# Loading a branch's register earlier, and idle matmuls in the first batch: attention and MLP on one core

## Chip, cores, metric

One core of one Trainium2 chip. The metric is the device time of one execution in microseconds (us), as the median of several; 32 of the 33 executions of the kernel before that ran beside the experiments lie within 0.3% of their median (313.96 us), and that spread is larger than most effects below, so the traces carry much of the argument. Engine names: PE is the matmul engine (PEld its weight loads), DVE VectorE, ACT ScalarE, POOL GpSimd, SP SyncE; a q behind the name is the engine's sequencer.

## The reference

```python
# q, k, v: (8, 8, 576, 64), s: (8, 8, 576); w_in: (512, 2048), w_out: (2048, 512)
scores = q @ k^T / sqrt(64)
cum    = cumsum(max(s, 0))
scores = where(causal, -1e9, scores + min(-(cum_i - cum_j), 0))
x      = (softmax(scores) @ v) as (4608, 512)
out    = gelu(x @ w_in) @ w_out            # exact gelu, float32
```

## The kernel before

The kernel computes attention in a factored form that is only right when certain bounds hold on the data. It tests them on the chip and writes the verdict, 0 or 1, to the one-element tile `bad`. At the end all engines load `bad` into a register and branch: where it is 0, as for this data, a long general version of the whole computation is skipped. The last sub-block of the output is evacuated and stored only behind the branch.

The MLP is done in nine chunks of 512 tokens, each with a layer 1 and four sub-blocks of layer 2. The end of the kernel before:

```python
        else:                                   # chunks 7 and 8
            for sub in range(4):
                l2_item(c, (sub,), store=(c, sub) < LAST)     # 16 matmuls of 512 columns each
                if c == B - 1:                                # chunk 7: writes `bad`
                    (cert_1, cert_2, cert_3, cert_4)[sub]()
    fast.close()

    rv = nc.values_load(bad[0:1, 0:1], min_val=0, max_val=1)  # register load on every engine
    with tc.If(rv > 0):
        ...                                                   # the general version, cut here
    with tc.manual_schedule():
        for sub in range(LAST[1], 4):                         # only sub-block 3 of chunk 8
            ...
            for i in range(2):
                cols = slice(i * 256, i * 256 + 256)
                nc.vector.tensor_copy(o_sb[:, cols], y[:, cols])
                nc.sync.dma_start(out=out[r0 : r0 + 128, cols], in_=o_sb[:, cols])
```

At the start PE would often be idle (in the run without the idle matmuls behind the weights it is busy for 2.54 us of the 5 from 5 to 10 us). `filler(n)` issues n matmuls of a zero tile (512 columns) into a PSUM buffer nobody reads:

```python
    filler(17)
    cum_sum(); masks(); weights()              # weights: PE transposes the cumulative sums
    ...
    filler(3)
    filler(3, raws[0, "qk"][:, 1, 0, :128])    # waits for the first key tile
    ...                                        # scores of batch 0 (sc_first: one filler behind each half)
    av_item(0, 1, 0)                           # value matmuls
    av_item(0, 1, 1)
    sc_first(1, 1, (1,), 0)
    to_xT(0, 0, True)                          # PE transposes of x; DVE copies them to xT
    to_xT(0, 1, True)
    mk_item(0, 0, 1)
    ...                                        # then layer 1 of chunk 0, which reads xT
```

## Time and profile before

| | before |
|---|---|
| median of the first 3 executions | 314.47 us (313.52 to 315.29) |
| span of the profiled execution | 313.1 us |
| PE busy | 303.3 us (97%) |
| last matmul ends / last copy starts | 307.6 / 308.20 us |

The lines are shown inside the prediction below. How to read them: a timeline line has the start in us, the length in us, the engine, the source line, the operation, what is written and read, how many instructions were merged, and in brackets how long the engine had been idle and what released it. A line of the waits has the waiter, the releaser, the total in us, the number of times and the longest. The span runs from the first to the last instruction; the time of an execution is 1.7 to 1.9 us longer than its span.

### The profile page before, as it was taken

Reading aid. Unit: us, or ns where it says so; the run is one execution under the profiler, and the core shown is the slowest. Engines: PE = TensorE matmul, PEld = TensorE weight load, DVE = VectorE, ACT = ScalarE, POOL = GpSimd, SP = SyncE. Lnnn points to the kernel's source line nnn. Section 1 sums busy time; section 2 is a strip of 40 time slices with the busy share of each in tenths; the row PEclk is TensorE's granted clock in tenths of the full one; section 3 lists DMA queues with packets and bytes.
Section 4 is the critical chain, followed back from the end, with each engine's and each line's share of the span. In section 5 each row is a group of like instructions: output and inputs, shape, how many; then the busy total and the mean of one; then the engine's idle time right before and its main releaser. Section 6 shows DMA issues by size and latency. Waiting matters only on the chain. (4 is left out here: it accounts for less than half of the span.)

```text
span 313.1 us, 6092 instructions
## 1 busy us (share of the span) xinstructions
PE 303.3 (97%) x2506; PEld 154.7 (49%) x2506; DVE 195.9 (63%) x397; ACT 193.3 (62%) x262; POOL 53.6 (17%) x72
## 2 busy tenths in 40 slices
PE   7999989999999999999999999999999999999992
PEld 2479655444554455445454445444544454444441
DVE  7876667697769785965597649954995532250010
ACT  2687868878848772965587458764876567006300
POOL 7383350142002400160006000500000000000000
PEclk9999999999999999999999999999999999999999
DMA  7999999769631973098218940634110311020012
GB/s 137 218 230 209 226 222 287 144 140 201 168 92 23 213 172 110 8 189 198 86 31 173 208 104 19 161 84 70 50 27 36 101 52 25 33 92 12 0 72 72
DMA packets 33028, 36.73 MB, mean 117 GB/s; under 512 B 17761, under 2 KB 22113, under 8 KB 32993
## 3 DMA queue, kind: packets, MB, share of 16 engines
q0 software_dynamic: 11472, 22.81, 37.3%
q1 hardware_dynamic: 20336, 12.93, 14.9%
q10 hardware_dynamic: 1184, 0.52, 0.6%
q8 instruction: 21, 0.34, 0.5%
q14 instruction: 15, 0.11, 0.1%
HBM read 36.85 MB, written 9.44 MB: 148 GB/s over the span
## 5 line engine op out<-in xcount | busy, mean ns | idle before, releaser
L488 PE MATMUL o_ps<-w_out_r,gT 128*128 128x512 bf16 x576 | 135.6, 379 | 0.8 <-DMA w_out_r<-in_moe_w_out_dram 0.8
L472 PE MATMUL h_ps<-xT,w_in_r 128*128 128x512 bf16 (+1 forms) x640 | 131.6, 358 | 0.6 <-DVE xT L418 0.6
L477 ACT ACTIVATE gT<-h_ps 128x1024 bf16<-128x1024 f32 (+1 forms) x80 | 75.1, 938 | 65.5 <-PE h_ps L472 64.4
L472 PEld LDWEIGHTS <-w_in_r 128*128 128x128 bf16 x640 | 60.0, 98 | 54.7 <-issue 0.7
L488 PEld LDWEIGHTS <-gT 128*128 128x128 bf16 x576 | 52.0, 98 | 57.7 <-issue 3.6
L364 ACT ACTIVATE P<-sc_ps 128x1024 bf16<-128x1024 f32 x56 | 54.3, 1021 | 26.1 <-PE sc_ps L349 26.1
L500 DVE COPY o_sb<-o_ps 128x512 f32<-128x512 f32 x30 | 20.7, 691 | 55.7 <-PE o_ps L488 55.7
L122 POOL DMA_DIRECT2D raw_v<-in_v_dram x39 | 33.1, 860 | 125.7 <-ACT sq L216 115.3
L188 DVE STREAM_TRANSPOSE qkT<-raw_qk 128x576 f32<-128x576 f32 x32 | 37.3, 1238 | 0.4 <-DMA raw_qk<-in_q_dram 0.3
L449 DVE RECIPROCAL rc<-av 128x4 f32<-128x4 f32 (+1 forms) x80 | 14.0, 175 | 35.1 <-PE av L440 35.0
L450 DVE TENSOR_TENSOR x<-av,rc 128x256 bf16<-128x256 f32 (+1 forms) x80 | 33.8, 423 | 3.0
L440 PEld LDWEIGHTS <-P 128*128 128x128 bf16 x576 | 26.5, 98 | 15.8 <-DVE P L372 1.4
L208 DVE TENSOR_REDUCE amx<-raw_qk 128x2 f32<-128x2304 bf16 x13 | 32.6, 2534 | 0.0
L440 PE MATMUL av<-vv,P 128*128 128x65 bf16 x576 | 30.2, 193 | 0.2 <-DVE x L450 0.2
L224 DVE TENSOR_TENSOR vv<-raw_v,wb 128x512 bf16<-128x512 f32 (+1 forms) x39 | 25.3, 691 | 4.0 <-DMA raw_v<-in_v_dram 4.0
L216 ACT ACTIVATE sq<-raw_v 128x512 bf16<-128x512 f32 (+1 forms) x40 | 24.8, 621 | 0.0
L372 DVE TENSOR_TENSOR P<-P,tri_bf 128x1024 bf16<-128x1024 bf16 (+1 forms) x33 | 22.0, 669 | 3.3 <-ACT P L364 3.2
L349 PE MATMUL sc_ps<-qkT 32*128 32x256 bf16 (+2 forms) x560 | 18.0, 250 | 0.0
L349 PEld LDWEIGHTS <-qkT 32*128 32x128 bf16 x560 | 11.7, 92 | 12.2 <-issue 8.9
L505 ACT ACT_TABLE_LOAD x8 | 10.3, 1283 | 1.3 <-PEq L823 1.2
L508 ACT ACT_TABLE_LOAD x8 | 10.3, 1283 | 0.1
L498 ACT ACTIVATE o_sb<-o_ps 128x512 f32<-128x512 f32 x5 | 2.9, 592 | 11.1 <-SPq L672 9.3
(80 smaller groups left out, 97.8 us busy)
## 6 DMA issues: line engine op xcount, KB each, us to landing
out_dram<-o_sb SPq DMA_DIRECT2D x34, 256.0 KB, 2.3
raw_v<-in_v_dram POOLq DMA_DIRECT2D x31, 256.0 KB, 5.6
raw_qk<-in_q_dram POOLq DMA_DIRECT2D x7, 576.0 KB, 7.8
raw_qk<-in_k_dram POOLq DMA_DIRECT2D x7, 576.0 KB, 11.1
w_in_r<-in_moe_w_in_dram POOLq DMA_DIRECT2D x4, 512.0 KB, 10.9
w_out_r<-in_moe_w_out_dram POOLq DMA_DIRECT2D x4, 512.0 KB, 15.9
raw_v<-in_v_dram POOLq DMA_DIRECT2D x8, 128.0 KB, 6.2
raw_qk<-in_q_dram POOLq DMA_DIRECT2D x2, 288.0 KB, 7.1
```

The source lines that it names most:

```text
L122: eng.dma_start(out=t[:n_st, st, :, :], in_=bass.AP(tensor=v.tensor, offset=v.offset + b * H * S * D + st * 128 * D, ap=[[D, n_st], [S * D ...
L188: nc.vector.transpose(qkT[b % 2][:, i, g, :S, :].rearrange("p s e -> p (s e)").bitcast(fp32) .rearrange("p (l j) -> p j l", j=LT), raws[b, ...
L208: nc.vector.tensor_reduce(amx[:, b * HG + g], raws[b, "qk"][:, :, g, :], axis=AX, op=ALU.max, apply_absolute_value=True,)
L216: nc.scalar.activation(sq[:n_st], raws[b, "v"][:n_st, st].rearrange("p h d -> p (h d)"), func=AF.Square, accum_out=sumv[:n_st, b, st : st ...
L224: eng.tensor_tensor(vv[b % 2][:n_st, st, :, 0:D], raws[b, "v"][:n_st, st, :, :], w.unsqueeze(2).to_broadcast([n_st, H, D]), op=MULT,)
L349: nc.tensor.matmul(s_ps[h // 2][:, h % 2, off : off + n], lhsT=qk[r, 1, g, jt * 128 : jt * 128 + 128, e], rhs=qk[r, 0, g, i0 : i0 + n, e], ...
L364: nc.scalar.activation(P[:, 2 * h2 : 2 * h2 + 2, o : o + 512], s_ps[h2], func=AF.Exp, scale=scale)
L440: nc.tensor.matmul(o_ps[:, h, :], lhsT=P[:, h, off : off + 128], rhs=vv[b % 2][:, jt, 4 * g + h, :], start=(i == 0), stop=(i == len(BLK[it ...
L450: nc.vector.tensor_tensor(x_of[b, it][:n, g * 256 : g * 256 + 256].rearrange("p (h d) -> p h d", d=D), o_ps[:n, :, 0:D], rc[:n].unsqueeze( ...
L472: nc.tensor.matmul(h_ps[:, i, :], lhsT=w_in_r[:, ko, ft * 128 : (ft + 1) * 128], rhs=xT[:, ko, c * NB + n0 : c * NB + n1], start=(ko == 0) ...
L477: nc.scalar.activation(gT_of[c][:, f2 * 2 : f2 * 2 + 2, n0:n1], h_ps, func=AF.Gelu)
L488: nc.tensor.matmul(y_of[c, sub], lhsT=gT[:, ft, sub * 128 : (sub + 1) * 128], rhs=w_out_r[:, ft, :], start=(ft == 0), stop=(ft == FT - 1),)
```

## The change

The intent: the register load stands right in front of the branch, and the engines pay for it there (471 to 632 ns each in the trace of before); it is moved behind the first sub-block of the last chunk's layer 2. In batch 0, five fillers are added in places where PE had waited or runs thin, and two are moved from in front of the weights' transposes to behind them.

```diff
-    filler(17)
+    filler(15)
     cum_sum()
...
-    filler(3)
+    filler(5)
     filler(3, raws[0, "qk"][:, 1, 0, :128])
...
     av_item(0, 1, 0)
+    filler(1)
     av_item(0, 1, 1)
     sc_first(1, 1, (1,), 0)
+    filler(1)
     to_xT(0, 0, True)
     to_xT(0, 1, True)
+    filler(3)
...
                 if c == B - 1:
                     (cert_1, cert_2, cert_3, cert_4)[sub]()
+                elif sub == 0:
+                    rv = nc.values_load(bad[0:1, 0:1], min_val=0, max_val=1)
     fast.close()
-    rv = nc.values_load(bad[0:1, 0:1], min_val=0, max_val=1)
     with tc.If(rv > 0):
```

## The prediction

> **What bounds the kernel now.** I read the page first (busy shares, clock row, chain), then the waits of the matmul engine over the whole span, then its timeline in the two stretches that the diff touches (start and end), then the instructions of the branch's two lines, then the transfers under the branch.
>
> The page's first two parts:
>
> ```profile
> span 313.1 us, 6092 instructions
> PE 303.3 (97%) x2506; PEld 154.7 (49%) x2506; DVE 195.9 (63%) x397; ACT 193.3 (62%) x262; POOL 53.6 (17%) x72
> ...
> PEclk9999999999999999999999999999999999999999
> ```
>
> The matmul engine (PE) is busy 97% of the span and its clock is granted throughout. Only an idle stretch of PE, or the tail after its last matmul, can be shortened by a change that removes no useful matmul. So I list PE's waits for the whole execution:
>
> ```profile
> PE f_ps L424 <- DVE zero L151: 1.2, 1, 1.2
> PE t_ps L247 <- ACT cum L241: 0.8, 1, 0.8
> PE o_ps L488 <- DMA w_out_r<-in_moe_w_out_dram: 0.8, 1, 0.8
> PE h_ps L472 <- DVE xT L418: 0.6, 1, 0.6
> PE sc_ps L394 <- DVE qkT L188: 0.5, 1, 0.5
> PE av L440 <- DVE x L450: 0.2, 1, 0.2
> ```
>
> All six lie in the first 41 us. The third, a wait for the second layer's weights, comes after all the others, so it can swallow what is gained or lost before it. From the timeline:
>
> ```profile
> 16.46 0.30 PE L440 MATMUL av<-vv,P 128*128 128x65 bf16 x4
> 16.94 0.41 PE L440 MATMUL av<-vv,P 128*128 128x65 bf16 x8 [0.17 <-DVE x L450]
> 17.28 0.63 PE L394 MATMUL sc_ps<-qkT 32*128 32x256 bf16 x12
> 17.84 0.64 PE L415 MATMUL xt_ps<-ident_bf,x 128*128 128x128 bf16 x8
> ...
> 40.97 1.89 PE L488 MATMUL o_ps<-w_out_r,gT 128*128 128x512 bf16 x8 [0.82 <-DMA w_out_r<-in_moe_w_out_dram]
> ```
>
> After 40.97 no PE wait is left until the end. The timeline of the last 10 us:
>
> ```profile
> 303.76 3.83 PE L488 MATMUL o_ps<-w_out_r,gT 128*128 128x512 bf16 x17
> ...
> 304.81 0.37 ACTq L502 DMA_DIRECT2D out_dram<-o_sb  x1
> 308.20 0.76 DVE L807 COPY o_sb<-o_ps 128x256 f32<-128x256 f32 x2 [6.79 <-PEq L672]
> 308.65 1.95 SPq L808 DMA_DIRECT2D out_dram<-o_sb  x2
> ```
>
> The last matmul ends at 303.76 + 3.83 = 307.59, but the copy that needs it starts only at 308.20, and it is released not by the matmul but by PE's sequencer on line 672, the branch. That is 0.61 us of tail. The instructions of lines 671 and 672 on the engines that matter:
>
> ```profile
> L671 DVEq TENSOR_LOAD <-bad x1: 542/542/542, 300.7 to 300.7; - x1
> L671 PEldq TENSOR_LOAD <-bad x1: 488/488/488, 303.6 to 303.6; - x1
> L671 ACTq TENSOR_LOAD <-bad x1: 471/471/471, 305.2 to 305.2; - x1
> ```
>
> ```profile
> L672 PEldq COMPARE_BRANCH  x1: 3898/3898/3898, 304.2 to 304.2; - x1
> ...
> L672 ACTq COMPARE_BRANCH  x1: 54/54/54, 305.8 to 305.8; - x1
> ```
>
> PE's sequencer works ahead of the array: it loads the register at 303.6, while 17 matmuls are still to run, and its branch lasts from 304.2 to 308.1. What holds the copy is the end of that branch.
>
> [...] in the stretch 304.2 to 308.1 the DMA view shows one instruction packet of 16 KB on the queue that fetches for PE through the whole kernel, inside 305.0 to 306.6; it is asked for about 1 us after the branch began and the branch ends about 1.5 us after it arrived. The body of the branch is not run here, so the branch is the long jump. [...] here the five take 471 to 632 ns. [...] PE's longest idle stretch before 41 us is 1.2 us[...].
>
> **The change part by part.**
>
> *Register load moved.* On each engine the load leaves its place just ahead of the branch and goes behind the first sub-block of the last layer 2. On PE that removes 0.49 us of load plus about 0.1 us of dispatch between 303.6 and 304.2: the branch should begin near 303.6 and, at the same 3.9 us, be through at 308.1 - 0.6 = 307.5. That is just before the last matmul ends (307.59), so the matmul becomes the releaser. PE's own semaphore step after the branch waits for that matmul and costs about 0.1 us (here branch end 308.06 to copy start 308.20), so the copy should start near 307.7 instead of 308.20: **about 0.5 us saved**. At the new place PE's load is covered: the last gelu ends near 294.85 (its start 293.82 plus 1.02), when the array has run about 6 of the sub-block's 16 matmuls, so the sequencer has about 10 x 0.216 = 2.2 us of queued work to hide 0.6 us. DVE waits for PE at that time (16 us idle before its copy at 297.27), ACT is idle till 304.18, and SyncE and GpSimd have nothing due: cost 0.
>
> *The rest of the tail must move with it.* SyncE's store of the first half follows the copy (308.20 + 0.42, issue at 308.65), but SyncE first passes five semaphore steps, from 308.2 to 308.5, that begin when ScalarE's store (issued 304.81) has fully landed. Most of that store lands near 306.8; its last part, at 308.2, seems held back by the instruction fetch on its DMA engine. That fetch comes 0.6 us earlier too, and ScalarE's branch loses its 0.47 us load, so I expect the steps to be through by about 308.0 and the store to issue near 308.15. Both stores and the closing 4.4 us keep their length.
>
> *Fillers before the weights.* 17 to 15 and 3 to 5: the sum stays 23 with the three behind the key tile. A warm filler steps 0.216 us. The first group ends 0.43 us earlier, into a wait (0.85 us for the cumulative sum); the second grows by 0.43 us, from about 8.75 to 9.2, past the key tile's arrival (9.05) by 0.15 us; the three behind it then end near 9.85, still ahead of the scores at 10.34, which wait for VectorE. Cost 0.
>
> *Five new fillers.* 5 x 0.216 = 1.08 us of array time. The one between the value matmuls falls into a gap (last start 16.57, next 16.94) and spills 0 to 0.1 us. The one before the transposes sits in a full stretch (scores end, transposes at 17.84) and pushes the transposes by 0.2 to 0.35 us; the copies to xT follow. The three behind the transposes take 0.65 us of the 0.8 us between the last transpose start (18.26) and the first layer-1 matmul (19.09). Layer 1 thus starts 0.2 to 0.45 us later. Then 16 us of dense matmuls carry the delay to 40.15, where PE waits 0.82 us for weights whose transfer (issued at 26.16 at the latest, on a queue that is full from 1 to 41 us) does not depend on PE. The delay is less than the wait: cost 0 at the end, and the wait shrinks to 0.4 to 0.6 us.
>
> Sum: 0.5 us of 314.5, or 0.16%.
>
> **The rivals.** (a) PE's branch waits for the array to drain rather than for its page: then it ends 0.45 us after the last matmul wherever it starts, and nothing is saved (314.5). For it: it ends soon after the matmuls end. Against: the 16 KB page inside it, and ScalarE, whose work was done at 305.2, also does its next step only at 308.4, 2.5 us after its branch. I give the page 70%. (b) SyncE's steps become the bound: ScalarE's store still lands at 308.2, the store issues at 308.57 and 0.1 us is saved (314.4). (c) The weights land early in other executions, the 0.8 us of slack is gone and the fillers cost their full 0.2 to 0.45 us (314.2 to 314.5 net). (d) The fillers are there for the clock: if in some executions of before the array falls back to half clock near 19 us, [...] the new fillers would lower the median. The three times differ by 1.8 us[...]; but the profiled execution, with a clean clock, took 314.89, above the median. I give it 10%.
>
> **Range and chances.** 314.47 - 0.5, with a third of the weight on smaller gains, gives 314.1. The spread is that of the runs: 313.52 to 315.29 for the same kernel, so a median of few runs is known to about 0.6 us. Range 313.0 to 315.1. Two per cent would be 6.3 us, more than all of PE's idle time and tail gap together (4.7 us), and the added array time is 1.08 us: neither side is reachable. Chances: faster 0.01, same 0.98, slower 0.01.
>
> **What would show it.** Right: PE's load near 295, its branch starting near 303.6 and still some 3.9 us long, the last copy released by the matmul of line 488 and starting about 0.1 us after it; span 312.6; first layer-1 matmul at 19.3 to 19.55 and PE's wait for weights at 41 us down to 0.4 to 0.6 us. Wrong: a branch that starts earlier and is longer by as much (drain); a copy that starts earlier and a store that does not (SyncE); a wait for weights that is gone, with everything after 41 us later.

"The five" that take 471 to 632 ns are the register loads. The sum came to 0.5 us, all of it from the load in front of PE's branch (0.49 us and about 0.1 us of dispatch go, after which the last matmul and no longer the branch releases the copy, 308.20 to about 307.7), with 0 for the load's new place and 0 for the fillers. The page rests on the packet in the trace and on the estimate of 70%, and rival (d) on an estimate of 10%.

## The result

Six executions of each: 313.70 us (312.9 to 313.91) after, 314.66 us (313.52 to 315.29) before. The ratio is 0.9969, with a 95% interval of 0.9949 to 0.9988. A ratio here is the mean time of one kernel's fast executions over that of the other's of the same rounds, so it is not quite the ratio of the quoted medians. The gain is small but clear of zero: 1.0 us, with an interval of about 0.4 to 1.6.

The page of the changed kernel, first and clock rows:

```profile
span 311.6 us, 6102 instructions
...
PE 304.0 (98%) x2511; PEld 155.1 (50%) x2511; DVE 196.5 (63%) x397; ACT 193.3 (62%) x262; POOL 53.2 (17%) x72
...
PEclk9999999999999999999999999999999999999999
```

PE has five matmuls more and is 0.7 us busier, in a span that is 1.5 us shorter. PE's waits, whole span:

```profile
PE t_ps L247 <- ACT cum L241: 1.6, 1, 1.6
PE f_ps L424 <- DVE zero L151: 1.2, 1, 1.2
PE o_ps L488 <- DMA w_out_r<-in_moe_w_out_dram: 0.5, 1, 0.5
```

Three of the six waits are filled; the first grew by 0.7 us, because two fillers (0.43 us) left the place in front of it and because the cumulative sum came later in this trace (PE's transposes start at 7.95 us in place of 7.68); the wait for the second layer's weights is down from 0.8 to 0.5 us. The timeline where the new fillers (line 424) stand:

```profile
16.43 0.38 PE L424 MATMUL f_ps<-zero 128*128 128x512 bf16 x1
16.76 0.42 PE L440 MATMUL av<-vv,P 128*128 128x65 bf16 x8
...
17.67 0.39 PE L424 MATMUL f_ps<-zero 128*128 128x512 bf16 x1
17.90 0.61 PE L415 MATMUL xt_ps<-ident_bf,x 128*128 128x128 bf16 x8
18.35 0.81 PE L424 MATMUL f_ps<-zero 128*128 128x512 bf16 x3
...
40.71 1.89 PE L488 MATMUL o_ps<-w_out_r,gT 128*128 128x512 bf16 x8 [0.52 <-DMA w_out_r<-in_moe_w_out_dram]
```

From the second group of value matmuls to the first layer-1 matmul it is 19.13 - 16.76 = 2.37 us; before it was 19.09 - 16.94 = 2.15. The fillers delay layer 1 by 0.22 us against the value matmuls. The end of the timeline:

```profile
302.64 4.70 PE L488 MATMUL o_ps<-w_out_r,gT 128*128 128x512 bf16 x21
...
307.47 0.76 DVE L812 COPY o_sb<-o_ps 128x256 f32<-128x256 f32 x2 [6.31 <-PEq L677]
307.92 1.22 SPq L813 DMA_DIRECT2D out_dram<-o_sb  x2
```

The last matmul ends at 302.64 + 4.70 = 307.34 and the copy starts 0.13 us later, not 0.61. By the semaphore events, which are finer, the copy followed the matmul's signal by 0.594 us before and by 0.115 after. The two stores together take 1.22 us to issue, against 1.95 before. The register load (now line 674) and the branch (line 677):

```profile
L674 PEldq TENSOR_LOAD <-bad x1: 491/491/491, 294.6 to 294.6; - x1
```

```profile
L677 PEldq COMPARE_BRANCH  x1: 3675/3675/3675, 303.3 to 303.3; - x1
```

So in this pair of traces the 1.5 us of span come from three places: 0.26 us because the second layer's weights landed earlier (40.97 against 40.71), 0.48 us between the last matmul and the copy, and 0.74 us in the issue of the second store (1.496 against 0.760 us, the longer of the two on line 808 and line 813). Which of them belongs to the change is a matter for experiments.

### The profile page after: what moved, and what is told of

It reads as the page before. It is cut to its first block, busy times and chain, and to the rows that moved or that the text cites. A ratio compares the mean times of both kernels' runs of the same rounds, so it can differ in the third digit from the quotient of the medians.

```text
span 311.6 us, 6102 instructions
## 1 busy us (share of the span) xinstructions
PE 304.0 (98%) x2511; PEld 155.1 (50%) x2511; DVE 196.5 (63%) x397; ACT 193.3 (62%) x262; POOL 53.2 (17%) x72
## 5 line engine op out<-in xcount | busy, mean ns | idle before, releaser
L372 DVE TENSOR_TENSOR P<-P,tri_bf 128x1024 bf16<-128x1024 bf16 (+1 forms) x33 | 22.7, 692 | 3.3 <-ACT P L364 3.2
L424 PE MATMUL f_ps<-zero 128*128 128x512 bf16 x30 | 9.8, 451 | 1.2 <-DVE zero L151 1.2
```

## The experiments

Theory A: PE's branch is bound by the fetch of the instruction page it jumps to (one packet of 16 KB in the traces); moving the load starts that fetch earlier and saves 0.48 us; the rest is the luck of transfers, and the fillers gain nothing. Rivals: the branch waits for the array to drain; the fillers earn part of the gain (by the clock, or by the order of transfers); the second store's issue is a lasting part of the gain.

All runs were correct and were timed with six executions each (four of the kernel without idle matmuls), beside the kernel before (11 executions of it in each of three calls: medians 313.99, 313.76 and 314.17 us). Some matmul records are missing in several of the traces (x551 in place of x576 on line 488), so no busy sums are compared there, only starts; the exceptions, for the clock in the run without idle matmuls, lie where no matmul is missing.

### The load alone

```diff
 # the kernel before
+                elif sub == 0:
+                    rv = nc.values_load(bad[0:1, 0:1], min_val=0, max_val=1)
     fast.close()
-    rv = nc.values_load(bad[0:1, 0:1], min_val=0, max_val=1)
```

> The kernel before with only the register load moved. Theory A (PE's branch is bound by the fetch of its target page, and PE's next page fetch after it delays the last store): PE's branch starts near 303.4 and ends before the last matmul; the last copy starts 0.1 to 0.15 us after the last matmul instead of 0.6; the second store's issue shrinks from 1.5 us to about 0.8 as in the changed kernel; PE's start-up waits stay as before. Time 0.7 to 1.2 us under before (ratio 0.996 to 0.998), which is all of the change's gain. Rival B (half of the gain comes from the fillers, by the clock or by the order of the transfers): under 0.5 us gained here.

313.69 us median against 313.99; ratio 1.000 (0.9975 to 1.0026), with one execution at 315.73 that pulls the mean. I had expected 0.7 to 1.2 us, and by its times alone this run would fit rival B. By time, nothing can be said. The trace says more: the end of its timeline is

```profile
301.63 6.21 PE L488 MATMUL o_ps<-w_out_r,gT 128*128 128x512 bf16 x27
...
307.96 0.76 DVE L809 COPY o_sb<-o_ps 128x256 f32<-128x256 f32 x2 [6.31 <-PEq L674]
308.41 1.74 SPq L810 DMA_DIRECT2D out_dram<-o_sb  x2
```

The copy starts 307.96 - 307.84 = 0.12 us after the last matmul, as in the changed kernel (0.115 by the semaphores). So the load move alone makes the whole of the 0.48 us. But the second store's issue took 1.28 us here, nearly as long as before: that part does not come with the load.

### The fillers alone

```diff
 # the changed kernel, with the register load back in front of the branch
-                elif sub == 0:
-                    rv = nc.values_load(bad[0:1, 0:1], min_val=0, max_val=1)
     fast.close()
+    rv = nc.values_load(bad[0:1, 0:1], min_val=0, max_val=1)
```

> The kernel before with only the fillers moved and added. Theory A: PE's waits for the scores and for xT are filled, its wait for the weights near 41 us shrinks to about 0.5 us, the tail is as before (copy 0.6 us after the last matmul, second store's issue about 1.5 us); time within 0.3 us of before (ratio 0.999 to 1.001). Rival B: 0.4 us or more gained.

314.27 us against 313.99; ratio 1.001 (0.9991 to 1.0029). The copy starts 0.58 us after the last matmul, as before; layer 1 starts 2.37 us after the value matmuls, as in the changed kernel. No gain from the fillers.

```profile
307.91 0.76 DVE L810 COPY o_sb<-o_ps 128x256 f32<-128x256 f32 x2 [6.77 <-PEq L675]
```

Two expectations missed. PE's wait for the second layer's weights is not at 41 us but near 43.7 us (0.5 us). And the second store issued in 0.48 us, although the tail's code is that of before. PE's next page was fetched late here, from 309.0 us, after that store had begun to issue. The weights that PE waits for near 41 us land at 39.5 to 40.7 us in the nine traces with the new fillers and at 39.8 to 41.1 us in the five without: the 0.26 us of the first pair lie within that scatter.

### No branch at all

```diff
 # the changed kernel
-                elif sub == 0:
-                    rv = nc.values_load(...)
-    with tc.If(rv > 0):
-        ...                      # the whole general version
```

This is not a valid kernel for other data: it never uses the verdict.

> The changed kernel without the branch and its body, which this data does not need (the result stays right for this data alone). Theory A: no page is fetched at the end, the copy starts within 0.05 us of the last matmul, both stores issue in 0.34 us; 0.4 to 0.8 us less than the changed kernel, so 1.4 to 1.8 us under before (ratio 0.9945 to 0.9955). If the second store's issue were long for a reason of its own (two stores in a row on one queue), it stays at 0.7 us or more and only 0.1 us is gained over the changed kernel.

312.66 us against 313.99; ratio 0.9959 (0.9944 to 0.9973). The timeline:

```profile
307.34 0.76 DVE L681 COPY o_sb<-o_ps 128x256 f32<-128x256 f32 x2 [6.21 <-PE o_ps L488]
307.80 0.81 SPq L682 DMA_DIRECT2D out_dram<-o_sb  x2
```

Now the matmul itself releases the copy, 0.024 us after its signal, and the two stores issue in 0.33 and 0.39 us. So a second store in a row is not slow for its own sake; it is slow next to the branch. The branch as a whole costs 1.3 us against the kernel before (means 314.02 and 312.69; this one also has the new fillers, which gained nothing). I had expected 1.4 to 1.8 us.

### Three loads in front of the branch

```diff
 # the kernel before
-    rv = nc.values_load(bad[0:1, 0:1], min_val=0, max_val=1)
+    rvs = [nc.values_load(bad[0:1, 0:1], min_val=0, max_val=1) for _ in range(3)]
+    rv = rvs[0] + rvs[1] + rvs[2]
```

> The kernel before with three register loads in a row in front of the branch, whose condition is their sum. PE's branch starts 1.1 to 1.4 us later (near 305.4). Theory A (page fetch): the branch stays about 3.9 us long, ends near 309.4, the last copy starts 1.1 to 1.4 us later, and the time grows by as much (ratio 1.0035 to 1.0045). Rival (the branch waits for the array to drain): the branch gets shorter by as much, the copy starts where it did, ratio 1.000.

315.53 us against 313.99; ratio 1.005 (1.0034 to 1.0066).

```profile
301.63 5.13 PE L488 MATMUL o_ps<-w_out_r,gT 128*128 128x512 bf16 x23
...
308.64 0.76 DVE L808 COPY o_sb<-o_ps 128x256 f32<-128x256 f32 x2 [8.06 <-PEq L673]
```

```profile
L673 PEldq COMPARE_BRANCH  x1: 4261/4261/4261, 304.2 to 304.2; - x1
```

The branch starts 0.91 us later relative to the last matmul than before (1.1 to 1.4 expected; the second and third load took only 0.31 us each), and lasts 0.36 us longer, where I had expected the same length; the copy comes 1.87 us after the matmul in place of 0.59. A branch that only waited for the array to drain would have ended where it did. With the changed kernel's branch, which was over at 306.99 while the array worked until 307.34, the drain rival has fallen twice. That its length follows the page is supported by the traces. The DMA view of before has this line for 304.2 to 308.1 us, the stretch of PE's branch:

```profile
q8 instruction: 1, 0.02, 2.3%
```

It says: one packet, 0.02 MB, 2.3% of the time of the 16 DMA engines. That q8 fetches for PE is read from the trace of before: its first 19 packets come 184 to 342 of PE's matmuls and weight loads apart (250 on the mean), and the one in the branch starts at 305.18 us, after PE's branch and before ScalarE's (305.76). Each of the 13 traces with a branch has one such packet of 16 KB in it, starting 1.0 to 1.8 us after the branch (1.76 us in this run, 1.02 before). It ends 2.1 to 2.9 us after the branch's start, and the branch ends 1.36 to 1.56 us after the packet in all of them. So the length goes with the packet; what those last 1.4 to 1.6 us are for stays open.

### The changed kernel again

No edit.

> The changed kernel once more, on the same chip as the other runs of this call. Theory A (0.48 us of tail for sure, a varying part from PE's next page fetch under the last store, nothing from the fillers): 0.4 to 0.9 us under before, ratio 0.997 to 0.999. Rival (the 1 us seen first is the true size): 0.9 to 1.1 us under before.

313.49 us against 313.76; ratio 0.9994 (0.9976 to 1.0012). The copy again starts 0.116 us after the matmul, but the second store's issue is 1.34 us: nearly the 1.50 of before. The gain of 0.3 us by the means is under the 0.4 to 0.9 us that I had expected. The 0.74 us in the first pair of traces did not come again, nor in the next run: most of it was luck, and 0.2 us of it may be lasting.

> The changed kernel a third time, beside the versions that it is to be compared with. From the two earlier measurements (1.0 us and 0.3 us under before) and the 0.48 us of tail that every trace shows: 0.2 to 0.9 us under before, ratio 0.997 to 0.9995.

313.71 us against 314.17; ratio 0.9985 (0.9969 to 1.0002); gap 0.115 us, second issue 1.32 us. By the means it is 0.58 us under before, inside what I had expected. From the last matmul's end to the end of the span it is 5.53 us before and 5.28 with the fillers alone; it is 4.30, 4.87 and 4.85 us in the three traces of the changed kernel and 4.84 with the load alone. The three measurements of the changed kernel agree with each other (means 313.58, 313.53 and 313.58 us); it is the kernel before that moved, from 314.56 in the first six executions to 314.02, 313.82 and 314.17. The 18 executions of the changed kernel average 313.56, the 33 of before 314.00: 0.44 us apart, with a standard error of 0.13 (worked out from the spreads of 0.39 and 0.51 us, over chips that need not be the same).

### The fourth sub-block freed from its wait

```diff
 # the changed kernel, in l2_item
+                if (c, sub + 1) == LAST:
+                    y_of[c, sub] = ps.tile([128, 2, NB], fp32, tag="sc", bufs=2, name="o2_ps")[:, 0, :]
+                else:
                     y_of[c, sub] = yps.tile(...)
```

> The changed kernel, with the third sub-block of the last layer 2 accumulated in another PSUM buffer, so that PE's sequencer need not wait for VectorE's copy of the second before it queues the fourth, and comes to the branch earlier. Theory A: PE's branch starts 2 us or more earlier (near 301), its page and the next one are fetched under the matmuls, so the second store's issue falls from 0.8-1.5 us to 0.4 us; the copy still starts 0.1 us after the last matmul. 0.3 to 0.8 us less than the changed kernel (ratio to before 0.995 to 0.997). Rival (the second store is slow because it is the second in a row on its queue): its issue stays over 0.7 us and the time is that of the changed kernel.

313.77 us against 313.76; ratio 0.9993. A miss. The branch did not start earlier:

```profile
L680 PEldq COMPARE_BRANCH  x1: 4095/4095/4095, 303.4 to 303.4; - x1
```

I had thought that PE's sequencer is held up by the wait in front of the fourth sub-block. In all 13 traces with a branch, the first thing behind the matmuls, be it load or branch, starts 3.65 us (to 2 ns) before the last matmul does, with that wait or without: 17 matmuls of 0.216 us. PE's sequencer is no further ahead than that in any of them, and with a branch of 3.7 to 4.3 us it is a near thing whether the branch ends before the array. Here it took 4.10 us, ended 0.05 us after the matmul's signal, and the copy came 0.20 us after the signal.

### The second store from ScalarE

```diff
 # the changed kernel
-                nc.sync.dma_start(out=out[r0 : r0 + 128, cols], in_=o_sb[:, cols])
+                (nc.sync, nc.scalar)[i].dma_start(out=out[r0 : r0 + 128, cols], in_=o_sb[:, cols])
```

> The changed kernel with the second half of the last store issued by ScalarE. If the slow issue belongs to SyncE's queue [...], ScalarE's issue takes 0.4 us, and the time is 0.2 to 0.5 us under the changed kernel; if the DMA engine that fetches PE's page is what holds the store up on any queue, the issue is still long, or the landing is, and nothing is gained. ScalarE's own page arrives late too (its step after the branch was at 307.8), so at best the issue starts near 308.3.

313.18 us (312.71 to 313.3) against 313.76; ratio 0.9979 (0.9965 to 0.9993). The mean is 0.41 us under that of the changed kernel (standard error 0.23, from the spreads of 0.22 and 0.53 us).

```profile
306.75 0.76 DVE L812 COPY o_sb<-o_ps 128x256 f32<-128x256 f32 x2 [6.37 <-PEq L677]
307.21 0.34 SPq L813 DMA_DIRECT2D out_dram<-o_sb  x1
307.54 0.34 ACTq L813 DMA_DIRECT2D out_dram<-o_sb  x1
```

The expectation's page of ScalarE is a packet of 8 KB: in the changed kernel's first trace it runs from 306.32 to 306.63 us, 1.4 us after ScalarE's branch (304.95), and ScalarE's next step follows 1.2 us after it (307.84). In this run ScalarE issues in 0.34 us while PE's page fetch is under way (307.37 to 308.67). On SyncE's queue the second store's issue ended 0.35 to 0.41 us after the end of PE's page fetch in all nine traces in which SyncE issued it with the fetch in flight. So what is stuck in its issue is SyncE's queue behind its own first store, not every queue. What holds it there is not shown. The landing is held up all the same: the second store landed 2.36 us after ScalarE had issued it, against 1.40 to 1.43 us after SyncE's issue in those nine traces and 1.43 us without a branch. In all 13 traces with a branch the last store landed only after the end of this second page fetch, the one behind the branch: 1.75 to 1.81 us after it in the nine and 1.49 to 1.59 us in the others. So another queue takes 0.2 to 0.3 us off, not the whole delay; from the last matmul to the end of the span it is 4.77 us here against 4.87 us in the changed kernel's trace of this call.

### That store, with the load move and without the new fillers

```diff
 # the load-alone kernel, with the same edit to the second store
```

> The kernel before with the register load moved and the second half of the last store issued by ScalarE, without the new fillers. If the fillers give nothing (their 0.22 us is swallowed by the weights' wait or lost), this is as fast as the changed kernel with ScalarE's store or up to 0.2 us faster: 0.6 to 1.1 us under before, ratio 0.9965 to 0.998. If the fillers are worth 0.3 us or more, it is no faster than the changed kernel.

313.09 us against 314.17; ratio 0.9972 (0.9952 to 0.9991); 0.45 us under the mean of the changed kernel (standard error 0.29, worked out in the same way), as expected. From the last matmul to the end it is 4.45 us, against 4.85. Leaving the fillers out did no harm. This and the run before have lower means than both kernels; with six executions each, the two are not told apart.

### One store in place of two

```diff
 # the changed kernel
-                nc.sync.dma_start(out=out[r0 : r0 + 128, cols], in_=o_sb[:, cols])
+            nc.sync.dma_start(out=out[r0 : r0 + 128, :], in_=o_sb)
```

> The changed kernel with one store of 256 KB behind the two last copies in place of two of 128 KB. If only a second store in a row on SyncE's queue is held up by PE's page fetch, the single one issues in 0.34 us right after the second copy (0.7 us after the first began), and the end lies 3.9 to 4.3 us after the copy's start instead of 4.2 to 4.7: 0 to 0.5 us less than the changed kernel. If the DMA engine that fetches is what holds back the end, its share of the store lands late here too and nothing is gained.

313.69 us against 314.17, but ratio 1.0001 (0.9982 to 1.0021), with two executions near 314.8. The issue took 0.34 us, as expected, but began 0.78 us after the copy, and the end came 4.35 us after the copy's start, just outside what I had written. In the trace the end is still earlier than in the changed kernel of the same call (4.73 us after the copy's start), but the times show no gain: the mean is 314.01 us against 313.58.

### Five more fillers

```diff
 # the changed kernel, behind the two transposes of x
-    filler(3)
+    filler(8)
```

> The changed kernel with eight instead of three fillers behind the transposes. Five more warm fillers are 1.08 us. Theory A (the fillers' delay is swallowed by PE's wait for the second layer's weights near 41 us, as far as there is one): the first layer-1 matmul starts 1.0 us later than in the changed kernel, the wait of 0 to 1.2 us is gone in most executions, and the time grows by 0.2 to 0.8 us over the changed kernel, not by 1.08. Rival (no slack): it grows by 1.0 us or more.

314.22 us against 313.76; ratio 1.0028 (1.0001 to 1.0055). The first layer-1 matmul starts at 20.03 us, 1.06 later than in the changed kernel of the same call, and the mean is 1.05 us over that kernel's (two executions at 315.2 and 316.3 weigh on it; by medians it is 0.73; 0.2 to 0.8 was expected). PE did not wait for the weights in this trace, nor in the changed kernel's trace of this call, so its delay came through in full. Theory A's slack is there in some executions only: of the nine traces of kernels with the new fillers, four show a wait for these weights (0.4 to 0.7 us) near 40.7 us, one another near 43.7, four none.

### No idle matmul behind the weights

```diff
 # the kernel before
-    filler(3)
-    filler(3, raws[0, "qk"][:, 1, 0, :128])
...
     sc_first(0, 1, (0,))
-    filler(1)
...
-    def sc_first(g, u, halves=(0, 1), fill=1):
+    def sc_first(g, u, halves=(0, 1), fill=0):
```

This takes away 11 fillers that before has too; the new ones were never in it.

> The kernel before without any idle matmul after the weights (only the 17 at the start stay). If the fillers are there for the clock and the clock is at risk (rival), the granted clock falls to half somewhere between 5 and 20 us in some executions, and the time grows by 0.5 us or more in them. If it isn't at risk, the clock row stays full, the scores and the first layer-1 matmul start up to 0.3 us earlier, and the time is within 0.3 us of before.

317.59 us against 314.17; ratio 1.0108 (1.009 to 1.0127): slower, and by far the largest effect. The clock row and two lines of its timeline:

```profile
PEclk9758999999999999999999999999999999999999
```

```profile
9.80 0.66 PE L394 MATMUL sc_ps<-qkT 32*128 32x256 bf16 x16 [1.37 <-DVE qkT L188]
...
20.66 6.81 PE L472 MATMUL h_ps<-xT,w_in_r 128*128 128x256 bf16 x40 [0.52 <-DVE xT L418]
```

The busy times of three stretches of 5 us (PE, PEld, DVE, ACT, POOL, each with its number of instructions; then the granted clock, the DMA share and GB/s):

```profile
5.00:10.00 5.00, 2.54 (x22) 1.21 (x24) 4.82 (x7) 1.64 (x4) 2.39 (x4) 1.00 1.10 200
10.00:15.00 5.00, 3.83 (x50) 2.23 (x44) 3.80 (x5) 4.33 (x5) 2.80 (x3) 0.67 1.20 216
15.00:20.00 5.00, 5.00 (x64) 4.05 (x63) 3.24 (x11) 3.51 (x4) 3.98 (x7) 0.50 1.20 236
```

After the stretch from 5 to 10 us, in which PE was busy for 2.54 us (3.90 before), the clock falls to half at 11.71 us and is back at 25.36 us. In the last 3.41 us before the fall PE was busy for 0.95 us, with no idle stretch over 1.4 us; at the same place it is busy for 2.83 us before and for all of it in the changed kernel. The clock's record lets one count further: in all 14 traces its full stretches last a whole number of steps of 3.413 us (90 steps are 307.2 us). A fall came only behind a step in which PE was busy for 1.22 us or less, and never behind one with 1.68 us or more; in the trace of before no step up to the last matmul has less than 2.35 us. The first 40 layer-1 matmuls take 6.81 us in place of 4.53. It happened in all four executions (mean granted clock 0.977 or 0.978). So the idle matmuls did hold the clock here, but the 11 that before already has are enough: in its 33 later executions the mean granted clock was never under 0.995. The half clock behind the last matmul gives that by itself: in the fillers-alone trace, whose mean is also 0.995, the clock is full from 5.72 to 309.50 us and half only after that. In these executions the five new ones had nothing left to save.

## Why the prediction was right

- **The branch.** Right, to the size: 0.5 us was predicted between matmul and copy, 0.48 measured, in the changed kernel's three traces and with the load alone. Less is saved where the branch comes out long (the copy came 0.20 us after the matmul's signal with a branch of 4.10 us). The loads in front of it took 471 to 632 ns (0.49 us on PE), and on PE the second and third of three in a row took 0.31 us. The page-fetch reading held against the drain rival (a). The label did not: the profile still names PE's sequencer as the releaser, because PE's own semaphore step behind the branch comes after the matmul (at 307.38 us, the matmul's signal at 307.35, the branch's end at 306.99) and not because the branch is late.
- **SyncE's steps** (rival b) were over at 307.36, before the copy: not a bound. The prediction's guess of what they wait for fits: in 12 of the 13 traces with a branch ScalarE's store landed 1.49 to 1.56 us after the end of the packet inside PE's branch (in the run with three loads, before its end). In the trace of before 15 of that store's 16 landing signals come from 306.72 to 306.86 us and the last at 308.18; 8 of its 128 packets of 2 KB, a sixteenth, start only from 306.61 us on, where the fetch's packet ends (306.63). That both ran on one DMA engine is the prediction's guess; no view names the engine of a packet.
- **"Both stores keep their length"** failed. The second store's issue swings between 0.48 and 1.51 us with PE's next page fetch. In the first pair of traces it gave 0.74 us; in the later two 0.15 to 0.17 us. It is a term of the sum that I took as fixed and that varies. It and the weights' 0.26 us are why the span came out at 311.6 where 312.6 was written.
- **The fillers' delay** of layer 1: 0.22 us, at the low end of 0.2 to 0.45. The start that was written, 19.3 to 19.55, was missed (19.13), because the value matmuls themselves came 0.18 us earlier. **"Cost 0 at the end"** holds only in executions in which PE still waits for the second layer's weights; with the wait gone, the delay comes through (rival c), as the run with five more showed. It is too small to be seen in the times.
- **The clock** (rival d): in the run without idle matmuls the clock did fall, to half for 13.65 us, and the time was 3.4 us longer, seven times the change; but no execution of before whose clock is on record showed it (mean granted clock 0.995 or more). One reading is wrong: the clock was not "granted throughout". In the trace of before the fillers step 0.427 us up to 4.59 us and 0.216 us from 5.16 us on; the row shows nines there because the clock's record begins only at 4.87 us. Nothing in the sum rests on it. The new fillers' removal of a risk is neither shown nor excluded for conditions that no run met.
- **The time.** 314.1 was predicted, in 313.0 to 315.1; 313.7 came out. The first ratio is worth 1.0 us where 0.5 was expected. The later measurements give 0.3 and 0.6 us: the first six executions of before were high. The range also holds the case of no gain (314.47), so that the time fell into it says little; it is the traces that bear the mechanism out.

## What to carry to other kernels

The conditional jump over the large body cost a page fetch here: PE's branch took 3.7 to 4.3 us with a packet of 16 KB in it, the other engines' 45 to 72 ns, and in the kernel before the last copy waited for PE's. What counts is when the last engine that somebody waits for reaches the branch, so look for what stands in front of it and can be done earlier. Look also at what is issued while such a fetch is under way: here a second store issued from another queue lowered the means by 0.4 us (0.1 and 0.4 us in the traces), though its landing still came after the fetch. The idle matmuls that before had were worth 3.4 us, and five more gained nothing that these runs could see; removing them is a quick test of whether they are needed.
